# Attention inside a fused kernel: blocks of 64 queries of two heads, Q block-diagonal, and V products over two tiles of queries at once

## The chip, the cores and the metric

The kernel runs on one core of a Trainium2 chip. The metric is device microseconds of one execution; the kernel before takes 874.42 us (median of 3 runs, 874.38 to 879.89).

## The reference

Three steps follow each other. First comes attention for 4 batches and 8 heads over 576 tokens of 64 numbers, in which a query sees all keys of its own block of 64 tokens and of the blocks before it. Then each of the 2304 tokens (512 numbers) is sent to one of 8 experts or skipped, and last comes a dense layer of width 2048. The attention is what the change touches:

```python
scores = scale * np.matmul(q, k.transpose(0, 1, 3, 2))
mask = (pos[:, None] // 64) >= (pos[None, :] // 64)
scores = np.where(mask, scores, -1000000000.0)
scores = scores - np.max(scores, axis=-1, keepdims=True)
attn = np.exp(scores)
attn = attn / (np.sum(attn, axis=-1, keepdims=True) + 1e-09)
return np.matmul(attn, v).astype(np.float32)
```

## The kernel before

The attention works on 16 pairs of heads (4 batches by 4 pairs), one pair after the other, with the stages of neighbouring pairs overlapped. The 576 tokens of a pair are cut into four tiles of 128 (tiles 0 to 3) and a last one of 64 (tile 4). Engines: TensorE (PE) does every product and transpose, VectorE (DVE) and ScalarE (ACT) take results out of PSUM, GpSimd (POOL) does small fills and the scattered writes of the routing, and SyncE (SP) issues the large transfers.

For each pair, `load` brings Q, K and V in (three buffers each), and `tr` turns Q and K over on PE (four transposes each, line 201), so that the two heads lie one above the other: head 0 on partitions 0 to 63, head 1 on 64 to 127. `split_qk` writes each as a high and a low part (lines 212 to 216), and scores are the sum of three products of such parts (line 236). `sc` makes the scores of one tile: for tile i the 128 queries of one head against the first n = 128(i+1) keys, three products for head 0 and three for head 1; each contracts over the 64 numbers of a head, so uses one half of the rows of the array. As a tile holds two blocks of 64, its first 64 queries may not see its last 64 keys; a product in bf16 of two small constants, `top` and `neg`, adds -2^30 there (line 238). Tile 4 is made otherwise: `qd` holds its 64 queries of both heads block-diagonally (head 0 in rows 0 to 63 and columns 0 to 63, head 1 in the other quarter, zeros elsewhere), so that one product with all 128 rows gives both heads (line 242).

`row_max` (line 249) takes the maximum of each row of a tile, `expo` (line 266) the exponential with its sum, head by head. `ptr` transposes the exponentials back in pieces of 128 by 128 (20 transposes per pair for tiles 3 to 0, line 296) and copies them to SBUF, mostly on ACT (line 274). `pv` multiplies them with V (line 315): for tile i and each block of 128 keys, one product for each head, with 64 columns of V stationary and 128 queries moving; the two heads write different halves of PSUM. An f32 product of this kind is two instructions, so that a pair has 40 of them. `pv` of tile 4 is line 308. `norm` and `xout` bring the result into the order of tokens.

The order is set by `OFF` and `at`: each step has a place on a line of 5 steps per pair (scores at 0, maximum 0.3, exponential 0.8, transposes 1.7, V product 2.5 steps after the start of a tile; tiles in the order 4, 3, 2, 1, 0; Q's transposes 3.6 steps ahead of the pair's first scores, the transposes of the 64-token tail 1.6 ahead, Q's and K's loads 10 and 9.5 ahead). That order gives priorities; a planner with its own costs arranges the instructions of each engine by them, and on the chip each engine runs its list in that order. From the 88th step on the order written is taken as it stands. Score tiles have two PSUM buffers (`ps_s`), transposes and small results share three (`ps_m`), the V product has one (`ps_o`). After the attention its buffers are given back, and only then do the weights of the third expert and later ones stream in through SP.

Of the kernel before, what the change touches and what calls it, by code (L numbers as in the profile page):

```python
# [9 lines left out]
F32 = mybir.dt.float32  # L10
F32R = mybir.dt.float32r
# [36 lines left out]
def tile_kernel(ctx: ExitStack, tc: tile.TileContext, q, k, v, w_skip, w_gate, w1, w2, w_in, w_out, alpha, out):  # L48
# [98 lines left out]
    top = acst.tile([128, 128], BF16, name="top")  # L147
    nc.vector.memset(top, 0.0)
    for r in (0, 64):
        nc.vector.memset(top[r:r + 1, 0:64], 1.0)  # L150
    neg = acst.tile([128, 64], BF16, name="neg")
    nc.vector.memset(neg, NEG)
# [33 lines left out]
    def load(p, nm, src):  # L186
        b, h0 = p // NP, p % NP * 2
        a = ld.tile([128, 5, 2, D], F32, tag=nm + "r", name=nm + "r")
# [9 lines left out]
    def tr(p, nm):  # L198
        ps = ps_m.tile([128, 512], F32, tag="m", name="ps" + nm)
        for t in range(4):  # L200
            nc.tensor.transpose(ps[:, t * 128:t * 128 + 128], tok4(p, nm, t), ident)
        for c in "hl":
            st[p][nm + c] = tp.tile([128, 512 if nm == "q" else S], F32R, tag=nm + c, name=nm + c)
# [14 lines left out]
    def tr_tail(p):  # L218
# [3 lines left out]
        for x, hs in enumerate(half):  # L222
            split_qk("q", *(qd[p % 2][hs, c, x * 64:x * 64 + 64] for c in range(2)), ps[hs, 0, :])
# [33 lines left out]
    def expo(p, i):  # L257
# [796 lines left out]
```

## Time and profile before

| | before |
|---|---|
| median of 3 runs | 874.42 us |
| profiled execution, time | 874.04 us |
| profiled execution, span | 872.4 us |
| PE busy | 809.5 us, 93% |
| DVE busy | 460.5 us, 53% |
| ACT busy | 302.8 us, 35% |
| POOL busy | 195.2 us, 22% |
| HBM read and written | 73.20 MB and 11.71 MB |

The span is that of the profiled execution, from its first instruction to its last; 1.6 us of its time lie outside. Busy times are over the whole span, in which the attention is the first 256 us, the experts follow until about 440 us and the dense layer takes the rest. The end of a matmul is modelled in this profile, so where times of PE are added up, starts are taken from starts.

### The profile page before, as it was taken

To read this page: it belongs to the slowest core of one execution; us is meant where nothing else is said; L and a number is where in the kernel's file an instruction comes from. 1 tells how busy PE (TensorE), PEld (TensorE's weight loads), DVE (VectorE), ACT (ScalarE), POOL (GpSimd) and SP (SyncE) were. 2 spreads that over 40 slices of the span, in tenths; PEclk is the share of its full clock that TensorE was granted. 3 is DMA by queue.
4 is the path that set the end of the run, shared out by engine and by line. 5 is a ranking of instruction groups with operands and counts; after the bars stand their busy time and mean duration, and the time that the engine had idled before them with its cause. 6 is when DMAs were issued, how large, how long until landed. Compare 5 with 4: busy or idle time off the path is not lost.

```text
span 872.4 us, 15135 instructions
## 1 busy us (share of the span) xinstructions
PE 809.5 (93%) x5804; PEld 622.0 (71%) x5804; DVE 460.5 (53%) x931; ACT 302.8 (35%) x793; POOL 195.2 (22%) x225
## 2 busy tenths in 40 slices
PE   7999999999995699999489987999999999999998
PEld 4777777777763565775268765788888888888897
DVE  4565757658555566798449999322322222222232
ACT  3766666666750222212134344311121112111121
POOL 1000110110204122323025556222122221212232
PEclk7999999999998799999699999999999999999999
DMA  6664354363314777784733222100020001000000
GB/s 126 163 190 131 85 138 108 84 164 104 98 56 109 242 234 252 235 285 133 235 114 120 89 72 73 48 1 1 1 97 1 1 1 48 25 1 1 25 25 25
DMA packets 96380, 85.86 MB, mean 98 GB/s; under 512 B 68601, under 2 KB 73913, under 8 KB 96272
## 3 DMA queue, kind: packets, MB, share of 16 engines
q1 hardware_dynamic: 93776, 78.88, 30.8%
q0 software_dynamic: 2496, 5.61, 2.1%
q8 instruction: 60, 0.98, 0.4%
q14 instruction: 48, 0.39, 0.2%
HBM read 73.20 MB, written 11.71 MB: 97 GB/s over the span
## 4 chain that ended last, share of the span: by engine, by line
PE 37%; DVE 12%; DMA 9%; issue 3%; ACT 1%; POOL 1%; SPq 0%; DVEq 0%; ACTq 0%; POOLq 0%
PE psf L955 18%; PE psa L988 6%; PE psa L987 6%; PE psa L997 6%; DMA w1t<-in_moe_w_dram 3%; DMA w2t<-in_moe_w_dram 3%; DVE dt L627 2%; DVE gt L966 2%; DMA dr<-in_moe_w_in_dram 2%; DVE dr L628 1%; DVE dt L631 1%; DVE dt L630 1%; DMA dr<-in_moe_w_out_dram 1%; DVE dt L629 1%; DVE wlo L618 1%
## 5 line engine op out<-in xcount | busy, mean ns | idle before, releaser
L955 PE MATMUL psf<-xs,whi 128*128 128x512 f32 (+1 forms) x640 | 160.6, 373 | 6.1 <-ACT xs L842 6.1
L973 POOL TENSOR_TENSOR gl<-gt,gh 128x512 fp32r<-128x512 f32 (+1 forms) x72 | 85.3, 1185 | 249.3 <-PE psa L997 135.9
L955 PEld LDWEIGHTS psf<-xs,whi 128*128 128x128 f32 x640 | 114.7, 188 | 31.3 <-ACT xs L842 6.7
L972 ACT ACTIVATE gh<-gt 128x512 fp32r<-128x512 f32 (+1 forms) x80 | 47.1, 588 | 255.5 <-PE psa L988 150.0
L968 DVE TENSOR_SCALAR gu<-psf,alf 128x512 f32<-128x512 f32 (+1 forms) x64 | 43.7, 683 | 165.2 <-PE psf L955 165.0
L955 PE MATMUL psf<-xs,wlo 128*128 128x512 f32 (+1 forms) x320 | 80.6, 374 | 0.0
L266 ACT ACTIVATE pe<-pss,mx 128x512 f32<-128x512 f32 (+3 forms) x128 | 66.4, 523 | 12.0 <-DVE mx L249 10.1
L249 DVE TENSOR_REDUCE mx<-pss 128x2 f32<-128x1024 f32 (+1 forms) x64 | 52.5, 820 | 31.2 <-PE pss L238 29.3
L955 PEld LDWEIGHTS psf<-xs,wlo 128*128 128x128 f32 x320 | 57.2, 189 | 12.0
L274 ACT ACTIVATE pt<-pspt 128x512 f32<-128x512 f32 (+3 forms) x112 | 52.0, 488 | 34.3 <-PE pspt L296 33.0
L987 PE MATMUL psa<-whi,gh 128*128 128x512 f32 x144 | 57.5, 400 | 4.0 <-ACT gh L972 4.0
L315 PE MATMUL pso<-pt,vr 128*64 128x128 f32 x640 | 59.7, 285 | 0.6 <-ACT pt L274 0.5
L987 PE MATMUL psa<-wkg,gh 128*128 128x512 f32 x144 | 56.8, 394 | 1.5 <-ACT gh L972 1.5
L988 PE MATMUL psa<-wlo,gh 128*128 128x512 f32 x144 | 56.3, 391 | 0.0
L988 PE MATMUL psa<-wkg,gh 128*128 128x512 f32 x144 | 56.2, 390 | 0.0
L296 PE MATMUL pspt<-ident,pe 128*128 128x128 f32 x320 | 52.5, 286 | 0.0
L969 DVE SCALAR_TENSOR_TENSOR gt<-psf,gu 128x512 f32<-128x512 f32 (+1 forms) x64 | 40.0, 625 | 11.5 <-POOL gl L973 5.4
L315 PEld LDWEIGHTS pso<-pt,vr 128*64 128x64 f32 x640 | 39.2, 136 | 9.5 <-issue 3.1
L843 DVE TENSOR_TENSOR xs<-psx,xs 128x512 fp32r<-128x512 f32 x18 | 12.4, 690 | 56.9 <-ACT xs L842 56.9
L296 PEld LDWEIGHTS pspt<-ident,pe 128*128 128x128 f32 x320 | 34.1, 140 | 11.1 <-issue 9.6
L627 DVE TENSOR_SCALAR dt<-dr 128x512 int32<-128x512 int32 x29 | 24.3, 838 | 33.2 <-DMA dr<-in_moe_w_in_dram 28.9
L692 PE MATMUL psh<-w1t,xts 128*32 128x256 f32 x256 | 21.1, 473 | 22.0 <-DMA w1t<-in_moe_w_dram 10.5
(237 smaller groups left out, 1470.3 us busy)
## 6 DMA issues: line engine op xcount, KB each, us to landing
w1t<-in_moe_w_dram SPq DMA_DIRECT2D x32, 512.0 KB
w2t<-in_moe_w_dram SPq DMA_DIRECT2D x32, 512.0 KB
dr<-in_moe_w_in_dram SPq DMA_DIRECT2D x16, 512.0 KB
dr<-in_moe_w_out_dram SPq DMA_DIRECT2D x16, 512.0 KB
out_dram<-ob SPq DMA_DIRECT2D x18, 256.0 KB
qr<-in_q_dram SPq DMA_DIRECT2D x32, 128.0 KB
kr<-in_k_dram SPq DMA_DIRECT2D x32, 128.0 KB
vr<-in_v_dram SPq DMA_DIRECT2D x32, 128.0 KB
```

What stands on the lines that cost most here:

```text
L249: nc.vector.tensor_reduce(out=m, in_=ps[:, :, 0:128 * i + 128], axis=AX.X, op=ALU.max, negate=True)
L266: ins = nc.scalar.activation(out=pt[:, x, 0:n], in_=ps[:, x, 0:n], func=AF.Exp, bias=m[:, x:x + 1], scale=1.0, accum_out=d["sum"][:, x * 4 ...
L274: nc.scalar.activation(out=o, in_=a, func=AF.Copy)
L296: nc.tensor.transpose(ps[:, y, j, :], e[:, x, j * 128:j * 128 + 128], ident)
L315: nc.tensor.matmul(d["o"][hs, i * 128:i * 128 + 128], v5[:, j, x, :], d["pt", i][:, x, j, :], start=(j == 0), stop=(j == i))
L955: nc.tensor.matmul(ps[:, 0:n], wsp[f // 4 * 4 + kk][a][:, ws], c[:, kk, 0:n], start=(n0 == 0 and kk == 0), stop=(n0 == 2 and kk == 3))
L968: nc.vector.tensor_scalar(out=u[:, 0:n], in0=ps[:, 0:n], scalar1=0.0, scalar2=alf[:, f:f + 1], op0=ALU.min, op1=ALU.mult)
L972: nc.scalar.activation(out=hi[:, 0:n], in_=t[:, 0:n], func=AF.Copy)
L973: (nc.gpsimd if w or f % 2 else nc.vector).tensor_tensor(out=lo[:, 0:n], in0=t[:, 0:n], in1=hi[:, 0:n].bitcast(F32), op=ALU.subtract)
L987: nc.tensor.matmul(o, hi[:, ts], whi, start=(f == 0), stop=False)
L988: nc.tensor.matmul(o, hi[:, ts], wlo, start=False, stop=False)
L997: nc.tensor.matmul(acc[w, t], lo[:, t * 128:t * 128 + 128], whi, start=False, stop=False)
```

## The change

Scores are now made in blocks of 64 queries of both heads. `qd`, the block-diagonal store, holds all nine blocks of a pair, with zeros written once at the start on POOL (2 by 2304 numbers per partition, where it was 2 by 256). `tr` of Q writes it in four instructions, two on ACT and two on DVE, each for the 64 partitions of one head, where it was one of each for 128. In `sc`, tile i consists of blocks 2i and 2i+1 (y = 0 and 1): three products of 128 rows for n = 128i+128 keys and three for n = 128i+64, so that no key that a query may not see is computed, and the product with `top` and `neg` goes. `row_max` and `expo` run by block, with the width of that block. The 64 keys that block 2i leaves out are filled with zeros in its exponentials by POOL (four fills a pair), so that the transposes stay as they were.

In `pv` the transposed exponentials of tiles 3 and 2 share one store, and those of 1 and 0 another; products for tile 3 and 1 alone go, and with tile 2 (and 0) one product covers 256 queries for each key block that both tiles have, and 128 for the last. The pair has 24 instructions on that line where it had 40. The result lies in another order of tiles, which `xout`, `weigh_all` and `route_last` follow. `norm` has four small copies where it had three. Q and K keep two load buffers instead of three.

```diff
-        a = ld.tile([128, 5, 2, D], F32, tag=nm + "r", name=nm + "r")
+        a = ld.tile([128, 5, 2, D], F32, tag=nm + "r", name=nm + "r", bufs=3 if nm == "v" else 2)
...
+        if nm == "q":
+            for x, hs in enumerate(half):
+                split_qk("q", *(qd[p % 2][hs, c, 0:8, x] for c in range(2)), ps[hs].rearrange("p (b n) -> p b n", b=8))
+            return
...
-    qd = [acst.tile([128, 2, 128], F32R, name=f"qd{n}") for n in range(2)]
+    qd = [acst.tile([128, 2, NB, 2, 64], F32R, name=f"qd{n}") for n in range(2)]
...
+        q2 = lambda a, blk: qd[p % 2][:, int(a == "ql"), blk].rearrange("p x n -> p (x n)")
         if i < 4:
-            n = 128 * i + 128
-            qc = slice(i * 128, i * 128 + 128)
-            for k, (a, b) in enumerate(PARTS):
-                for x, hs in enumerate(half):
-                    nc.tensor.matmul(ps[:, x, 0:n], d[a][hs, qc], d[b][hs, 0:n], start=(k == 0), stop=False)
-            for x, hs in enumerate(half):
-                nc.tensor.matmul(ps[:, x, n - 64:n], top[hs], neg[hs], start=False, stop=True)
+            for y in (1, 0):
+                n = 128 * i + 64 + 64 * y
+                for k, (a, b) in enumerate(PARTS):
+                    nc.tensor.matmul(ps[:, y, 0:n], q2(a, 2 * i + y), d[b][:, 0:n], start=(k == 0), stop=(k == 2))
...
-            nc.vector.tensor_reduce(out=m, in_=ps[:, :, 0:128 * i + 128], axis=AX.X, op=ALU.max, negate=True)
+            for y in (1, 0):
+                nc.vector.tensor_reduce(out=m[:, y:y + 1], in_=ps[:, y, 0:128 * i + 64 + 64 * y], axis=AX.X, op=ALU.max, negate=True)
...
-            n = 128 * i + 128
-            for x in range(2):
-                ins = nc.scalar.activation(out=pt[:, x, 0:n], in_=ps[:, x, 0:n], func=AF.Exp, bias=m[:, x:x + 1], scale=1.0, accum_out=d["sum"][:, x * 4 + i:x * 4 + i + 1])
+            nc.gpsimd.memset(pt[:, 0, 128 * i + 64:128 * i + 128], 0.0)
+            for y in (1, 0):
+                n = 128 * i + 64 + 64 * y
+                ins = nc.scalar.activation(out=pt[:, y, 0:n], in_=ps[:, y, 0:n], func=AF.Exp, bias=m[:, y:y + 1], scale=1.0, accum_out=d["sum"][:, 2 * i + y:2 * i + y + 1])
...
-        o = d["pt", i] = ptp.tile([128, 2, i + 1, 128], F32, tag="pt", name="pt", padded_shape=[128, 2, 4, 128])
+        g, first = i // 2, i % 2
+        if first:
+            n = 7 if g else 3
+            d["pt", g] = ptp.tile([128, n, 2, 2, 64], F32, tag=f"pt{'ab'[1 - g]}", name="pt", bufs=1 + g)
+        o = d["pt", g]
...
+            r = slice(1 - first, 2 * i + 2 - first, 2)
+            copy((f"{i}{'ab'[xs[0]]}" if i > 1 else str(i)) in ON_ACT, o[:, r, xs[0]:xs[-1] + 1].rearrange("p n y x c -> p y n (x c)"), ps)
...
-        for j in range(i + 1):
+        c0 = 256 - i * 128
+        pt = d.pop(("pt", i // 2))
+        for j in range(i + 2):
+            n = 2 if j <= i else 1
             for x, hs in enumerate(half):
-                nc.tensor.matmul(d["o"][hs, i * 128:i * 128 + 128], v5[:, j, x, :], d["pt", i][:, x, j, :], start=(j == 0), stop=(j == i))
+                nc.tensor.matmul(d["o"][hs, c0:c0 + n * 128], v5[:, j, x, :], pt[:, 2 * j:2 * j + n, :, x].rearrange("p n y c -> p (n y) c"), start=(j == 0), stop=(j == i + 1))
```

## Rows read from the trace of the kernel before

**Rows 1.** The page: engines' busy time, and PE's granted clock in 40 slices.
```profile
PE 809.5 (93%) x5804; PEld 622.0 (71%) x5804; DVE 460.5 (53%) x931; ACT 302.8 (35%) x793; POOL 195.2 (22%) x225
...
PEclk7999999999998799999699999999999999999999
```

**Rows 2.** Table by stretch: us, busy us (instructions) of PE, PEld, DVE, ACT, POOL; clock; DMA.
```profile
120.00:140.00 20.00, 19.55 (x183) 14.41 (x183) 13.27 (x27) 13.44 (x41) 1.16 (x2) 1.00 0.37 89
...
200.00:220.00 20.00, 19.96 (x244) 15.11 (x243) 15.72 (x60) 13.17 (x43) 1.36 (x6) 1.00 0.37 105
```

**Rows 3.** PE's timeline from 119.87 us: start, duration, line, shape, count, [idle before].
```profile
119.87 0.50 PE L236 MATMUL pss<-kh,qh 64*128 64x512 f32 x2
...
123.52 0.66 PE L339 MATMUL psx<-ident,xt 128*128 128x128 f32 x4 [0.23 <-DVE xt L276]
...
125.71 0.95 PE L308 MATMUL pso<-pt,vr 128*64 128x64 f32 x20
126.59 1.09 PE L296 MATMUL pspt<-ident,pe 128*128 128x128 f32 x8
```

**Rows 4.** PE's timeline from 131.90 us on, ending one pair after rows 3 began.
```profile
131.90 0.66 PE L296 MATMUL pspt<-ident,pe 128*128 128x128 f32 x4
132.31 0.48 PE L242 MATMUL pss<-kh,qd 128*128 128x512 f32 x1
132.63 0.40 PE L242 MATMUL pss<-kl,qd 128*128 128x512 f32 x1
132.86 0.42 PE L242 MATMUL pss<-kh,qd 128*128 128x512 f32 x2
133.12 0.28 PE L242 MATMUL pss<-kl,qd 128*128 128x64 f32 x1
133.23 0.28 PE L242 MATMUL pss<-kh,qd 128*128 128x64 f32 x1
133.44 0.66 PE L315 MATMUL pso<-pt,vr 128*64 128x128 f32 x8
134.02 0.44 PE L296 MATMUL pspt<-ident,pe 128*128 128x128 f32 x2
134.39 0.50 PE L236 MATMUL pss<-kh,qh 64*128 64x512 f32 x2
134.73 0.39 PE L236 MATMUL pss<-kl,qh 64*128 64x512 f32 x2
134.96 0.39 PE L236 MATMUL pss<-kh,ql 64*128 64x512 f32 x2
135.20 0.20 PE L238 MATMUL pss<-neg,top 64*128 64x64 bf16 x2
135.33 0.66 PE L201 MATMUL psq<-ident,qr 128*128 128x128 f32 x4
135.92 0.44 PE L315 MATMUL pso<-pt,vr 128*64 128x128 f32 x4
```

**Rows 5.** Groups by shape, 0 to 250 us: busy us, mean ns, idle before.
```profile
L249 DVE TENSOR_REDUCE mx<-pss 128x2 f32<-128x1024 f32 x16 | 19.6, 1225 | 14.7 <-PE pss L238 14.6
...
L214 DVE SCALAR_TENSOR_TENSOR ql<-psq,qh 128x512 fp32r<-128x512 f32 x16 | 11.1, 691 | 5.0 <-ACT qh L212 4.7
...
L249 DVE TENSOR_REDUCE mx<-pss 128x2 f32<-128x256 f32 x15 | 6.3, 423 | 9.4 <-PE pss L238 9.4
...
L212 ACT ACTIVATE qh<-psq 128x512 fp32r<-128x512 f32 x16 | 9.6, 597 | 11.1 <-PE psq L201 11.1
...
L369 POOL MEMSET lw<- 128x72 f32 x4 | 0.6, 156 | 8.0 <-DVE l L409 8.0
...
L208 POOL MEMSET qd<- 128x256 f32 x2 | 0.5, 302 | 0.0
```

**Rows 6.** PE's timeline, the last result of the attention.
```profile
256.08 0.66 PE L339 MATMUL psx<-ident,xt 128*128 128x128 f32 x4 [0.80 <-DVE xt L276]
```

**Rows 7.** SP's timeline, the first weights issued after the attention.
```profile
275.50 6.26 SPq L79 DMA_DIRECT2D w2t<-in_moe_w_dram  x4
```

More of the change, by code (lines that the diff above doesn't have):

```diff
@@ L146, in tile_kernel @@
     nc.vector.tensor_scalar(out=tlo, in0=tok, scalar1=63, scalar2=None, op0=ALU.bitwise_and)
[L147 to L152, printed above, removed]
     thi = acst.tile([128, 5], F32, name="thi")
@@ L201, in tr @@
             nc.tensor.transpose(ps[:, t * 128:t * 128 + 128], tok4(p, nm, t), ident)
+        if nm == "q":
+            for x, hs in enumerate(half):
+                split_qk("q", *(qd[p % 2][hs, c, 0:8, x] for c in range(2)), ps[hs].rearrange("p (b n) -> p b n", b=8))
+            return
         for c in "hl":
-            st[p][nm + c] = tp.tile([128, 512 if nm == "q" else S], F32R, tag=nm + c, name=nm + c)
+            st[p][nm + c] = tp.tile([128, S], F32R, tag=nm + c, name=nm + c)
         split_qk(nm, *(st[p][nm + c][:, 0:512] for c in "hl"), ps)
-    qd = [acst.tile([128, 2, 128], F32R, name=f"qd{n}") for n in range(2)]
+    qd = [acst.tile([128, 2, NB, 2, 64], F32R, name=f"qd{n}") for n in range(2)]
     for n in range(2):
@@ L222, in tr_tail @@
         for x, hs in enumerate(half):
-            split_qk("q", *(qd[p % 2][hs, c, x * 64:x * 64 + 64] for c in range(2)), ps[hs, 0, :])
+            split_qk("q", *(qd[p % 2][hs, c, 8, x] for c in range(2)), ps[hs, 0, :])
         split_qk("k", *(st[p]["k" + c][:, 512:S] for c in "hl"), ps[:, 1, :])
@@ L241, in sc @@
                 for k, (a, b) in enumerate(PARTS):
-                    nc.tensor.matmul(o, qd[p % 2][:, int(a == "ql")], d[b][:, c], start=(k == 0), stop=(k == 2))
+                    nc.tensor.matmul(o, q2(a, 8), d[b][:, c], start=(k == 0), stop=(k == 2))
     def row_max(p, i):
@@ L296, in ptr @@
                     nc.tensor.transpose(ps[:, y, j, :], e[:, x, j * 128:j * 128 + 128], ident)
-            copy((f"{i}{'ab'[xs[0]]}" if i > 1 else str(i)) in ON_ACT, o[:, xs[0]:xs[-1] + 1], ps)
+            r = slice(1 - first, 2 * i + 2 - first, 2)
+            copy((f"{i}{'ab'[xs[0]]}" if i > 1 else str(i)) in ON_ACT, o[:, r, xs[0]:xs[-1] + 1].rearrange("p n y x c -> p y n (x c)"), ps)
     def pv(p, i):
@@ L327, in norm @@
         nc.vector.reciprocal(out=r, in_=r)
-        nc.vector.tensor_copy(out=rb[b][:, 0:4, hp, :], in_=r[:, 0:8].rearrange("p (x t) -> p t x", x=2))
         for x, hs in enumerate(half):
-            nc.vector.tensor_copy(out=rb[b][0:64, 4, hp, x:x + 1], in_=r[hs, 8:9])
+            for y, rows in enumerate(half):
+                n = 5 - y
+                nc.vector.tensor_copy(out=rb[b][rows, 0:n, hp, x:x + 1], in_=r[hs, y:9:2].unsqueeze(2))
     def xout(p):
@@ L338, in xout @@
         for t in range(4):
-            nc.tensor.transpose(ps[:, t].rearrange("p h d -> p (h d)"), xt[:, t * 128:t * 128 + 128], ident)
+            nc.tensor.transpose(ps[:, t].rearrange("p h d -> p (h d)"), xt[:, 384 - t * 128:512 - t * 128], ident)
         if hp % 2 == 0:
@@ L385, in weigh_all @@
         for t in range(4):
-            nc.tensor.transpose(ps[:, t, 0:n].rearrange("p h c -> p (h c)"), lg[0:n * 32, t * 128:t * 128 + 128], ident[0:n * 32, 0:n * 32])
+            nc.tensor.transpose(ps[:, t, 0:n].rearrange("p h c -> p (h c)"), lg[0:n * 32, 384 - t * 128:512 - t * 128], ident[0:n * 32, 0:n * 32])
         for t in range(4):
@@ L397, in route_last @@
             kk = 128 if t < 4 else 64
-            nc.tensor.matmul(ps[0:kk, t, 0], xts[b * NP + hp][:, t * 128:t * 128 + kk], wbd[:, hp, 0:18], start=True, stop=True)
+            c0 = 384 - t * 128 if t < 4 else 512
+            nc.tensor.matmul(ps[0:kk, t, 0], xts[b * NP + hp][:, c0:c0 + kk], wbd[:, hp, 0:18], start=True, stop=True)
         f = rb[b][:, 0:4, hp].unsqueeze(3).to_broadcast([128, 4, 2, 9])
```

4 lines of the change are left out of this document (3 added, 1 removed).

## The prediction

> **What bounds the kernel now.** I read the page first, then a table by stretch, then PE's timeline of one pair, then the groups by shape, and last how the attention ends and what starts after it. On the page PE is busy for 93% of the span and no other engine for more than 53%, and PE's granted clock stands in its top tenth in the slices of the steady attention [rows 1]; the table gives it there as 1.00, the 2.4 GHz level [rows 2]. In those stretches PE is busy for 19.55 and 19.96 of 20 us, DVE for 13.27 and 15.72, ACT for some 13.4, POOL for about 1 [rows 2]. So PE sets the pace of the attention. The busy share does not say whether PE streams or drains, so I add starts.
>
> One pair lasts from 119.87 to 134.39, the same product of tile 3 in both rows: 14.52 us [rows 3, 4]. There are 16 such pairs, and the routing lies among them. Within a stretch of equal shapes a transpose costs 0.11: two transposes between other work take 0.37 (134.02 to 134.39), four take 0.59 (135.33 to 135.92), hence 0.11 each and a constant of 0.15 [rows 4]. Eight V instructions take 0.58 (133.44 to 134.02): four couples of heads at 0.11 and again a constant of 0.14 [rows 4]. This constant is what a reader should see: it appears where PE passes between products of 128 rows and columns (transposes, tile 4's scores), products of 64 rows (the other scores) and products of 64 columns (V). Where transposes pass to tile 4's scores it is missing: 131.90 to 133.44 holds four transposes, three products of 512 at 0.23 and three of 64 at 0.11, 1.46 in all, against 1.54 shown with an entry and an exit in it [rows 4]. From 119.87 to 134.39 the timeline passes 21 times between the three kinds, rows 3 giving the first and rows 4 the last.
>
> **The change, part by part.** All figures are per pair in us unless said.
>
> Scores, streaming. Two heads of 64 rows run side by side: both products of 512 (134.73) are followed by the next two after 0.23, which is what one product of 128 rows takes (132.63 to 132.86) [rows 4]. So before, tiles 3 to 0 cost three times 0.23, 0.17, 0.12 and 0.11: by columns at 0.45 ns, with 0.11 as the floor (133.12 to 133.23) [rows 4]; together 1.89. After, the blocks run one behind the other: 512, 448, 384, 320, 256, 192, 128 and 64 columns at 0.23, 0.20, 0.17, 0.14, 0.12 and three times 0.11, 1.19 for each of three parts, 3.57. That adds 1.68. The Trainium skill, "TensorEngine Tiling (Array Packing)", section "Theoretical Speedup", says that splitting the array's rows for contractions of at most 64 gives up to 2x; by it alone this change gives half of the array away, and the sum would be these 1.68 a pair, 25 us more in 15 pairs. The rows agree on the streaming, and the rest of the sum is what that rule leaves out.
>
> Masks. Four couples go. One takes 0.13 up to the next work (135.20 to 135.33) [rows 4], of which I count 0.07 as its own, the rest is the way out of the stretch: -0.28.
>
> Switches. The first score after a switch also takes 0.34 instead of 0.23 (134.39 to 134.73) [rows 4], 0.05 above the constant; six such entries fall away, -0.30. In the order of the steps, after the change, only V of tiles 0 and 1, V of tile 4, the 64-row transposes of the tail, and V of tiles 2 and 3 interrupt the full shape: 8 switches instead of 21, -13 x 0.15 = -1.95. Before, that written order has 16; the planner made 21 by cutting V of tile 3 and scores in pieces. A cut of V in the new order costs two switches, 0.30.
>
> V products. Columns stay: 20 couples of 128 (2.20) become 8 of 256 and 4 of 128, the same at equal price per column. The moving operand now lies in runs of 64. Bounds: nothing, or the price of separate products of 64, (0.88 - 0.25)/10 = 0.06 against 0.055 from tile 4's V (125.71 to 126.59, of which I count 0.25 as its constant and the way to its last products of 64 rows) [rows 3], +0.2. I take nothing, as a couple of 256 issues fewer instructions.
>
> Sum: +1.68 - 0.28 - 0.30 - 1.95 = -0.85. Adding the whole pair as a test: 38 transposes 4.18, V 2.20, V of tile 4 0.88, tile 4's scores 1.02, tail 0.2, scores 1.89, masks 0.28, twenty switches 3.0 (one is in the 0.88), entries 0.30, the wait for the copied result 0.23 [rows 3]: 14.18 of 14.52. The missing 0.34 is couples broken by other work, which can't happen to blocks, and small waits. Against that I allow one cut of V at 0.30. I take -0.8; ends: -1.4 (no cut, no leftover waits) and 0 (three cuts).
>
> DVE. Q's low part takes two instructions of 0.69 instead of one; eight maxima replace four: from 1225 ns for 1024 columns and 423 for 256 a column costs 1.04 ns and an instruction 0.16 [rows 5], so 4 x 0.16 more less 256 columns, +0.37; one small copy in norm, 0.15 at most. Together +1.2. ACT: one more instruction of 0.60 [rows 5], less narrower exponentials. Both lie beside PE's work. If the cover goes, PE waits for maxima or copies: this is a rival below. Latency per tile does not grow, as the exponential of one block can start while the next block is still multiplied.
>
> POOL. Four fills a pair, each below the 156 ns of a fill of 72 columns [rows 5], are covered by the exponentials that run at the same time. They stand in POOL's queue with the tokens that release weight loads and with the list writes, which wait for K or an exponential; what is behind them then is a fill, and behind that PE's transposes, planned 0.9 step later than the exponential. Bounds 0 to 0.6; I take 0. Filling the larger store at the start: 302 ns for 256 columns, 156 for 72 [rows 5], 0.8 ns a column, 1.9 us each, once, before PE has turned Q over a second time; 0.
>
> Loads. With two buffers Q of the pair after next can be issued once the tail of the pair using that buffer is turned over, eight steps (some 23 us) ahead of its own transposes; SP issues in order, so a waiting Q load holds V loads and weights behind it. Bounds 0 and one late load; I take 0.
>
> Ends. At the start nothing overlaps Q's second instructions: up to 0.60 + 0.69 [rows 5], taken +0.8. At the end the last V product comes in one group and its copy is waited for as today (0.80) [rows 6]: +0.3. The weights after the attention are issued at 275.50, behind its end [rows 7], so that the later stages move with it and the gain is kept whole.
>
> The pairs at the two ends overlap only half, so 15 x -0.8 = -12.0; with the ends -10.9. The profiled execution takes 874.04, 1.6 outside its span of 872.4; the median is 0.4 above it. **874.0 - 10.9 = 863.**
>
> **Rivals.**
> 1. *A larger gain.* V is never cut, and the leftover waits go as well: -1.4 x 15 + 1 = -20, 854. For it: five stretches of one kind merge into one another. Against it: the planner cut V before.
> 2. *DVE (with ACT) becomes the bound.* Scaled to a pair, DVE has 9.6 to 11.4 us of work [rows 2], with 1.2 more 10.8 to 12.6, in a pair of 13.7: 79 to 92%. With queues in order and the routing in bursts, PE then waits on maxima and the gain shrinks to between 0 and 0.4 a pair: 869 to 875. Against it: ACT and DVE have a fifth of their time free away from the routing.
> 3. *Slower: the switches stay.* V's group needs the last copies of tile 2 (or 0), and the planner may cut it into pieces and put scores between. Place: V against the full shape; price 0.30 a cut. From three cuts a pair the gain is gone; with all 21 switches it is -0.85 + 1.95 = +1.1 a pair, 874 + 16.5 + 1 = 892; with five cuts +0.65, 885. The skill's rule named above points this way too. For it: today's 16 became 21. Against it: most of those cuts were scores, which are now of one shape with the transposes.
>
> **How the numbers follow.** About 1%, 8.7 us, is what can be told from no change. Forecast, 857 to 870: 0.55, two thirds of it faster by over 1%, as the bound lies at 865.7. Rival 1: 0.18. Rival 2: 0.15, within 1%. Rival 3: 0.12, nearly all slower by over 1%. Faster: 0.37 + 0.18 = 0.55; same 0.18 + 0.15 + 0.01 = 0.34; slower 0.11. The range takes most of rival 1 and rival 2 and leaves the far end of rival 3: 850 to 878.
>
> **What would show it.** One pair of PE's timeline should hold 8 to 12 stretches and last some 13.7; tiles' scores as 128-row products 0.23 apart for 512 columns, with no constant beside transposes; V in groups of 16 and 8 instructions, about 1.7 and 0.8 with their constants; the list of waits with little of DVE or POOL before PE. Wrong would be: a gap between transposes and block scores, V in four or more pieces, PE idle behind a maximum or a fill, or a first weight issued after the attention that doesn't move with its end.

## The result and the profile after

The changed kernel takes 881.26 us (median of 15 runs, 879.36 to 887.01) and the kernel before, run beside it, 876.35 (15 runs): a ratio of 1.0058, with a 95% interval of 1.0037 to 1.0079. The forecast was 863 us with a range of 850 to 878, so it was wrong, and in its sign. The profiled execution took 882.70 us, with a span of 881.1.

The page of the kernel after, the line of busy times and that of PE's granted clock, answering to [rows 1]:

```profile
PE 797.8 (91%) x5420; PEld 623.5 (71%) x5420; DVE 480.8 (55%) x1023; ACT 311.9 (35%) x809; POOL 207.3 (24%) x289
...
PEclk7999999999997899999699999899999999999999
```

PE has 11.7 us less to do than before and the span is 8.7 us longer: the gain in work is there, and more than all of it has gone into idle time. The table by stretch of the kernel after (us, then busy us and instructions of PE, PEld, DVE, ACT, POOL; clock; DMA), in the two stretches of [rows 2]:

```profile
120.00:140.00 20.00, 18.54 (x156) 14.90 (x152) 12.79 (x35) 13.44 (x41) 3.05 (x9) 1.00 0.43 101
200.00:220.00 20.00, 18.99 (x186) 14.83 (x186) 15.83 (x61) 13.30 (x39) 1.17 (x8) 1.00 0.45 128
```

The granted clock is 1.00 in both stretches, as before, so there it is not the clock. PE was idle for 0.45 and 0.04 of these 20 us; now it is idle for 1.46 and 1.01. PE's timeline of one pair of the kernel after (start, duration, line, shape, count, [idle before <- what ended it]) shows where:

```profile
64.56 0.66 PE L348 MATMUL psx<-ident,xt 128*128 128x128 f32 x4 [0.22 <-ACT pt L272]
...
67.10 0.95 PE L311 MATMUL pso<-pt,vr 128*64 128x64 f32 x20 [0.58 <-DVE xr L355]
...
71.49 1.74 PE L323 MATMUL pso<-pt,vr 128*64 128x256 f32 x16 [0.66 <-ACT pt L272]
73.16 0.66 PE L298 MATMUL pspt<-ident,pe 128*128 128x128 f32 x4
...
74.59 0.44 PE L298 MATMUL pspt<-ident,pe 128*128 128x128 f32 x2
74.79 0.47 PE L234 MATMUL pss<-kh,qd 128*128 128x512 f32 x1
75.10 0.39 PE L234 MATMUL pss<-kl,qd 128*128 128x512 f32 x1
75.33 0.60 PE L234 MATMUL pss<-kh,qd 128*128 128x512 f32 x2
75.76 0.36 PE L234 MATMUL pss<-kl,qd 128*128 128x448 f32 x1
...
76.70 0.87 PE L323 MATMUL pso<-pt,vr 128*64 128x256 f32 x8
77.50 0.66 PE L283 MATMUL pspt<-ident,p 128*128 128x128 f32 x4
...
79.45 0.33 PE L348 MATMUL psx<-ident,xt 128*128 128x128 f32 x1 [0.22 <-ACT pt L272]
```

This pair lasts 14.89 us (64.56 to 79.45), and 13.43 of them are PE's own work. Two waits are new: 0.58 before V of tile 4, for DVE's `xr`, and 0.66 before V of tiles 3 and 2, for ACT's copy of transposes. The pair of [rows 3] passed V of tile 4 without a wait (125.71), but only just, as DVE's timeline of the kernel before shows; the second part of `xr` ends at 125.71 there:

```profile
125.44 0.27 DVE L347 TENSOR_TENSOR xr<-psx,rb 64x128 f32<-64x128 f32 x1
```

DVE's timeline of the kernel after, ahead of the first wait, tells what made `xr` late:

```profile
62.73 0.68 DVE L212 SCALAR_TENSOR_TENSOR qd<-psq,qd 64x512 fp32r<-64x512 f32 x1
63.34 0.67 DVE L274 COPY xt<-pso 128x512 f32<-128x512 f32 x1
63.94 0.67 DVE L274 COPY pt<-pspt 128x512 f32<-128x512 f32 x1
64.64 0.69 DVE L212 SCALAR_TENSOR_TENSOR qd<-psq,qd 64x512 fp32r<-64x512 f32 x1
65.37 0.95 DVE L246 TENSOR_REDUCE mx<-pss 128x1 f32<-128x384 f32 x2
66.35 0.69 DVE L355 TENSOR_TENSOR xr<-psx,rb 128x512 f32<-128x512 f32 x1
```

From 62.73 on DVE has no pause: the second half of Q's low part (64.64, 0.69 us) stands ahead of two maxima and of `xr`. V of tile 4 needs one of the three shared PSUM buffers (`ps_m`), and the one it gets is held by the transposes that `xr` (66.35) reads. So the 0.58 at PE is most of that 0.69; the first run below takes it away. An instruction on 64 partitions costs what one on 128 does: 0.68 and 0.69 here, 691 ns before [rows 5]. For the second wait, ACT's timeline of the kernel after:

```profile
70.56 0.87 ACT L272 ACTIVATE pt<-pspt 128x384 f32<-128x384 f32 x2
```

Both copies of tile 2 run on ACT (70.56), the second right behind the first, and the group of 16 V instructions starts at 71.49 when the later is done. Before, V of tile 3 ran by itself ahead of these copies, and V of tile 2 began without a wait, as PE's timeline of the kernel before shows:

```profile
130.85 1.12 PE L315 MATMUL pso<-pt,vr 128*64 128x128 f32 x12
```

The list of waits from 20 to 240 us of the kernel after (who waits, for whom: us in total, times, longest; PEld is PE's load of a stationary operand, which waits just ahead of its product):

```profile
POOL pe L261 <- PE pspt L298: 80.7, 47, 3.4
...
PEld pso L311 <- DVE xr L355: 9.1, 13, 0.8
...
PEld pso L323 <- ACT pt L272: 5.4, 7, 0.8
```

The first wait comes in 13 pairs, the second in 7. POOL's fills wait for PE for 80.7 us in all, and no row has PE waiting for a fill. Finally the end of the attention, from PE's timeline, and the first weights behind it, from SP's, of the kernel after:

```profile
263.19 0.66 PE L348 MATMUL psx<-ident,xt 128*128 128x128 f32 x4 [0.79 <-DVE xt L274]
```
```profile
283.00 1.02 SPq L79 DMA_DIRECT2D w2t<-in_moe_w_dram  x2
```

The attention ends 7.1 us later than in [rows 6] and the weights start 7.5 later than in [rows 7]; the span is 8.7 longer, so most of the loss lies in the attention. Of its 7.1 us, 1.1 come before the first result (34.76 instead of 33.69). Over 12 pairs (second to fourteenth result) a pair takes 15.67 us on average instead of 15.20; idle time of PE in it is 1.40 instead of 0.18, and the rest 14.27 instead of 15.02.

### The profile page after: what moved, and what is told of

It is laid out like the page before. It is cut to its first block, busy times and chain, and to the rows that moved or that the text cites. A ratio compares the mean times of both kernels' runs of the same rounds, so it can differ in the third digit from the quotient of the medians.

```text
span 881.1 us, 14573 instructions
## 1 busy us (share of the span) xinstructions
PE 797.8 (91%) x5420; PEld 623.5 (71%) x5420; DVE 480.8 (55%) x1023; ACT 311.9 (35%) x809; POOL 207.3 (24%) x289
## 4 chain that ended last, share of the span: by engine, by line
PE 51%; DVE 19%; DMA 12%; ACT 9%; issue 4%; SPq 1%; POOL 1%; another core or an unknown queue 1%; DVEq 0%; ACTq 0%; POOLq 0%
PE psf L965 18%; PE psa L998 6%; PE psa L997 6%; PE psa L1007 6%; DMA w1t<-in_moe_w_dram 4%; DMA w2t<-in_moe_w_dram 4%; PE pss L234 4%; ACT pe L264 3%; PE pso L323 3%; ACT pt L272 3%; DMA dr<-in_moe_w_in_dram 2%; PE pspt L298 2%; DVE mx L246 2%; DVE dt L637 2%; ACT qd L210 2%
## 5 line engine op out<-in xcount | busy, mean ns | idle before, releaser
L234 PE MATMUL pss<-kh,qd 128*128 128x512 f32 (+7 forms) x256 | 76.0, 340 | 2.5 <-ACT pe L264 2.1
L264 ACT ACTIVATE pe<-pss,mx 128x512 f32<-128x512 f32 (+7 forms) x128 | 63.2, 498 | 10.5 <-DVE mx L246 8.1
L246 DVE TENSOR_REDUCE mx<-pss 128x1 f32<-128x512 f32 (+7 forms) x128 | 53.4, 449 | 19.6 <-PE pss L234 18.4
L234 PEld LDWEIGHTS pss<-kh,qd 128*128 128x128 f32 x256 | 47.0, 192 | 7.4 <-ACT pe L264 3.5
L323 PE MATMUL pso<-pt,vr 128*64 128x256 f32 (+1 forms) x384 | 41.7, 352 | 6.0 <-ACT pt L272 6.0
L979 DVE SCALAR_TENSOR_TENSOR gt<-psf,gu 128x512 f32<-128x512 f32 (+1 forms) x64 | 40.0, 625 | 10.2 <-POOL gl L983 4.0
```

The lines of the kernel that those rows point to most:

```text
L234: nc.tensor.matmul(ps[:, y, 0:n], q2(a, 2 * i + y), d[b][:, 0:n], start=(k == 0), stop=(k == 2))
L246: nc.vector.tensor_reduce(out=m[:, y:y + 1], in_=ps[:, y, 0:128 * i + 64 + 64 * y], axis=AX.X, op=ALU.max, negate=True)
L264: ins = nc.scalar.activation(out=pt[:, y, 0:n], in_=ps[:, y, 0:n], func=AF.Exp, bias=m[:, y:y + 1], scale=1.0, accum_out=d["sum"][:, 2 * i ...
L323: nc.tensor.matmul(d["o"][hs, c0:c0 + n * 128], v5[:, j, x, :], pt[:, 2 * j:2 * j + n, :, x].rearrange("p n y c -> p (n y) c"), start=(j = ...
```

## The experiments

Theory: what PE saves is lost to Q's second instructions, which delay `xr` and the maxima on DVE and copies on ACT. Rivals: the blocks themselves cost PE more than forecast, the V groups wait for copies whatever Q does, or the PSUM buffer, not engine time, is what Q's second instructions use up. All ratios are to the kernel before on the same chip, with 95% intervals. "Pair" is the distance between the third and fourth result on PE, idle time of PE that within this pair, and "passages" counts how often PE passes in it between the three kinds of products that the prediction names. "First" and "last" are the times at which PE starts the first and the sixteenth result, in the one profiled execution of each run.

| run | ratio | interval | pair, us | idle, us | passages | first, us | last, us |
|---|---|---|---|---|---|---|---|
| before | 1 | | 14.52 | 0.22 | 21 | 33.69 | 256.08 |
| after | 1.0058 | 1.0037 to 1.0079 | 14.89 | 1.45 | 8 | 34.76 | 263.19 |
| e1_q_once | 0.9877 | 0.9850 to 0.9904 | 13.93 | 0.80 | 8 | 32.72 | 248.25 |
| e14_act_twice | 0.9926 | 0.9901 to 0.9952 | 14.05 | 0.80 | 8 | 33.31 | 250.25 |
| e15_dve_twice | 1.0015 | 0.9989 to 1.0042 | 14.86 | 1.46 | 8 | 32.36 | 258.94 |
| e10_q_second_from_sbuf | 1.0009 | 0.9985 to 1.0033 | 14.89 | 1.50 | 8 | 32.13 | 258.07 |
| e9_before_q_halves | 1.0144 | 1.0105 to 1.0183 | 15.35 | 1.00 | 21 | 34.44 | 269.47 |
| e4_v_groups_only | 0.9869 | 0.9848 to 0.9890 | 13.57 | 0.36 | 14 | 32.34 | 243.48 |
| e16_v_groups_2b | 0.9874 | 0.9831 to 0.9916 | 13.19 | 0.36 | 14 | 32.63 | 243.08 |
| e8_v_groups_swapped | 0.9872 | 0.9832 to 0.9912 | 13.12 | 0.00 | 16 | 38.51 | 253.68 |
| e3_blocks_only | 1.0184 | 1.0164 to 1.0204 | 15.31 | 1.17 | 12 | 35.28 | 271.42 |
| e13_blocks_pool | 0.9902 | 0.9864 to 0.9940 | 14.34 | 0.51 | 12 | 30.05 | 248.90 |
| e2_copies_swapped | 0.9987 | 0.9959 to 1.0015 | 14.10 | 0.76 | 8 | 35.47 | 259.43 |
| e6_q_by_pool | 0.9846 | 0.9803 to 0.9890 | 13.93 | 0.80 | 8 | 28.56 | 243.66 |
| e7_q_by_dma | 1.0117 | 1.0075 to 1.0158 | 13.44 | 0.61 | 10 | 34.79 | 272.22 |
| e11_pool_swapped | 0.9803 | 0.9767 to 0.9839 | 13.42 | 0.25 | 8 | 28.79 | 241.00 |
| e12_pool_2b | 0.9786 | 0.9741 to 0.9832 | 13.53 | 0.41 | 8 | 29.15 | 240.95 |

**Q's second instructions.** The first run takes them out of the changed kernel:

```diff
-            for x, hs in enumerate(half):
-                split_qk("q", *(qd[p % 2][hs, c, 0:8, x] for c in range(2)), ps[hs].rearrange("p (b n) -> p b n", b=8))
+            split_qk("q", *(qd[p % 2][:, c, 0:8, 0] for c in range(2)), ps.rearrange("p (b n) -> p b n", b=8))
```

> The changed kernel, but Q's high and low part are each written by one instruction for all 128 partitions into the same half of the block-diagonal store, so that the two heads' queries mix (the separation of the heads is left out; PE's work is the same). Theory A (PE waits for DVE and ACT): DVE reaches the copy of the result (xr) 0.69 us earlier and the 0.58 us that PE waits for it in each pair goes: 881 - 9 = 872 us. Theory B (block scores and V groups cost PE more than was priced): no change, 881 us.

Measured 868.69 us, 0.9877. Two instructions a pair, one on each engine and both off the path by their engines' busy shares, cost 1.8% (1.0058 against 0.9877), three times the loss that was to be explained. In PE's timeline of this run only one wait is left in the pair, that for tile 2's copies, as long as in the kernel after; so this one belongs to the V groups and not to Q:

```profile
66.93 1.74 PE L322 MATMUL pso<-pt,vr 128*64 128x256 f32 x16 [0.66 <-ACT pt L271]
```

The next run puts Q's second instructions into the kernel before, where nothing else is changed:

```diff
-        split_qk(nm, *(st[p][nm + c][:, 0:512] for c in "hl"), ps)
+        for hs in half if nm == "q" else [slice(0, 128)]:
+            split_qk(nm, *(st[p][nm + c][hs, 0:512] for c in "hl"), ps[hs])
```

> The kernel before with Q's high and low part written by two instructions each for 64 partitions, nothing else changed. Theory A (DVE is on PE's path at xr): xr ends at 125.71 in the kernel before, just when PE starts the product that needs its PSUM buffer, so that DVE's 0.69 more a pair shows almost whole: +0.4 to +0.6 a pair, 884 to 887 us, 1.007 to 1.010 of before. Rival (the halves cost only together with the blocks' additional maxima): no change, within 0.3%.

Measured 890.24 us, 1.0144, more than I expected. DVE's timeline of this run, the kernel before with Q in halves, shows the same picture as that of the kernel after:

```profile
65.62 0.69 DVE L215 SCALAR_TENSOR_TENSOR ql<-psq,qh 64x512 fp32r<-64x512 f32 x1
66.34 0.96 DVE L250 TENSOR_REDUCE mx<-pss 128x2 f32<-128x768 f32 x1
67.33 0.69 DVE L347 TENSOR_TENSOR xr<-psx,rb 128x512 f32<-128x512 f32 x1
```

And PE's timeline of the same run waits twice in the pair, for a copy on ACT and for `xr`:

```profile
65.45 0.66 PE L340 MATMUL psx<-ident,xt 128*128 128x128 f32 x4 [0.62 <-ACT pt L275]
...
68.08 0.95 PE L309 MATMUL pso<-pt,vr 128*64 128x64 f32 x20 [0.37 <-DVE xr L347]
```

So the cost does not need the blocks: a schedule in which `xr` came just in time has no room for 0.69 us ahead of it. Two runs divide it between the engines, each with one instruction on one of them for all 128 partitions and two on the other:

```diff
             for x, hs in enumerate(half):
-                split_qk("q", *(qd[p % 2][hs, c, 0:8, x] for c in range(2)), ps[hs].rearrange("p (b n) -> p b n", b=8))
+                nc.scalar.activation(out=qd[p % 2][hs, 0, 0:8, x], in_=pv_(ps[hs]), func=AF.Copy, scale=0.125)
+            for x, hs in full:        # full = [(0, slice(0, 128))]; in e15 it stands above, and half here
+                nc.vector.scalar_tensor_tensor(out=qd[p % 2][hs, 1, 0:8, x], in0=pv_(ps[hs]), scalar=0.125, in1=qd[p % 2][hs, 0, 0:8, 0].bitcast(F32), op0=ALU.mult, op1=ALU.subtract)
```

> The changed kernel with Q's high part written by two instructions on ACT as it is there, the low part by one on DVE for all 128 partitions (the heads' separation is left out). If it is DVE's 0.69 a pair that PE waits for, this takes the time of e1, 867 to 870 us, 0.988 of before; if it is ACT's 0.60, that of the changed kernel, 880 to 883, 1.006; if both count, 873 to 877.

> The reverse: the high part by one instruction on ACT, the low part by two on DVE (the heads' separation is left out). If it is DVE's 0.69 a pair that PE waits for, the time of the changed kernel, 880 to 883 us, 1.006 of before; if ACT's 0.60, that of e1, 867 to 870, 0.988; if both count, 873 to 877.

Measured 871.35 us, 0.9926, and 880.66, 1.0015. Against e1, ACT's second instruction costs 0.5% and DVE's 1.4%, in sum about the 1.8% of both. With DVE's alone the idle time is back at 1.46. One more run keeps the engine time of both and lets the PSUM buffer go, as the second instructions read SBUF:

```diff
-            for x, hs in enumerate(half):
-                split_qk("q", *(qd[p % 2][hs, c, 0:8, x] for c in range(2)), ps[hs].rearrange("p (b n) -> p b n", b=8))
+            split_qk("q", *(qd[p % 2][:, c, 0:8, 0] for c in range(2)), ps.rearrange("p (b n) -> p b n", b=8))
+            hs = half[1]
+            hi, lo = (qd[p % 2][hs, c, 0:8] for c in range(2))
+            nc.scalar.activation(out=hi[:, :, 1], in_=hi[:, :, 0].bitcast(F32), func=AF.Copy, scale=0.125)
+            nc.vector.scalar_tensor_tensor(out=lo[:, :, 1], in0=hi[:, :, 0].bitcast(F32), scalar=0.125, in1=hi[:, :, 1].bitcast(F32), op0=ALU.mult, op1=ALU.subtract)
```

> The changed kernel with as many instructions for Q on ACT and DVE as it has, but the first of each covers all 128 partitions and reads PSUM, and the second, for 64 partitions, reads SBUF (the heads' separation is left out). Theory A1 (the second instructions hold one of the three shared PSUM buffers longer, and PE waits for a buffer): the time of e1, 0.988 of before, 867 to 870 us. Theory A2 (it is DVE's and ACT's time, 0.69 and 0.60 a pair ahead of what PE waits for): that of the changed kernel, 1.006, 880 to 884 us. In between, the share of each.

Measured 879.85 us, 1.0009, between the two theories. The steady pair is that of the kernel after (14.89 us, of which 1.50 idle instead of 1.45), so in it the engines' time counts, and letting the buffer go earlier gains nothing. This run is 0.5% faster than the kernel after all the same. In the profiled executions its attention ends 5.1 us earlier, of which 2.6 come before the first result; whether the PSUM buffer has a part in that is not shown.

**V and the blocks, each alone.** The kernel before with the V groups (and two load buffers for Q and K), its scores and its Q as they were:

```diff
-        o = d["pt", i] = ptp.tile([128, 2, i + 1, 128], F32, tag="pt", name="pt", padded_shape=[128, 2, 4, 128])
+            d["pt", g] = ptp.tile([128, n, 2, 128], F32, tag=f"pt{'ab'[1 - g]}", name="pt", bufs=1 + g)
...
-                nc.tensor.matmul(d["o"][hs, i * 128:i * 128 + 128], v5[:, j, x, :], d["pt", i][:, x, j, :], start=(j == 0), stop=(j == i))
+                nc.tensor.matmul(d["o"][hs, c0:c0 + n * 128], v5[:, j, x, :], pt[:, 2 * j:2 * j + n, x], start=(j == 0), stop=(j == i + 1))
```

> The kernel before with V products for two tiles at once, scores as before (two heads side by side, with the mask product). Theory A: five or six V stretches become two, at 0.30 each -0.9 to -1.2 us a pair, and a wait for tile 2's copies of up to 0.7 comes in: -0.2 to -1 a pair, 876 - 3 to - 15, so 861 to 873 us. Rival C (grouping V is what costs): 876 + 5 to + 10, 881 to 886 us.

Measured 866.6 us, 0.9869. The groups alone gain 1.3%. PE's timeline of this run, from one result to the next:

```profile
59.47 0.65 PE L348 MATMUL psx<-ident,xt 128*128 128x128 f32 x4
...
65.41 2.11 PE L324 MATMUL pso<-pt,vr 128*64 128x256 f32 x16 [0.23 <-ACT pt L274]
...
73.03 0.66 PE L348 MATMUL psx<-ident,xt 128*128 128x128 f32 x4
```

The wait for tile 2's copies is there with 0.23 instead of 0.66, and V of tile 4 waits for nothing. Fourteen passages between kinds remain of 21, and the pair is 0.95 shorter. The blocks without the groups, with Q as in the change:

```diff
-            d["pt", g] = ptp.tile([128, n, 2, 2, 64], F32, tag=f"pt{'ab'[1 - g]}", name="pt", bufs=1 + g)
+        o = d["pt", i] = ptp.tile([128, 2, i + 1, 2, 64], F32, tag="pt", name="pt", padded_shape=[128, 2, 4, 2, 64])
...
-                nc.tensor.matmul(d["o"][hs, c0:c0 + n * 128], v5[:, j, x, :], pt[:, 2 * j:2 * j + n, :, x].rearrange("p n y c -> p (n y) c"), start=(j == 0), stop=(j == i + 1))
+                nc.tensor.matmul(d["o"][hs, c0:c0 + 128], v5[:, j, x, :], pt[:, :, j, x], start=(j == 0), stop=(j == i))
```

> The changed kernel with V products tile by tile as before the change (40 instructions a pair), scores in blocks. Theory A: V of tile 3 no longer waits for tile 2's copies, which gives back up to 0.66 us a pair, but three more V stretches cost six switches at 0.15: 0 to +0.9 a pair, 881 to 890 us. Rival C (grouping V is what costs, since it waits for the later of two tiles): 881 - 10 = 871 us.

Measured 894.51 us, 1.0184, outside what was expected: by itself this half of the change is slower than the whole change. But it holds Q's second instructions. The same with Q spread by POOL (as in e6 below):

> e3 (scores in blocks, V tile by tile) with Q's copies by POOL as in e6. Without the second instructions on ACT and DVE the blocks should cost what they were priced at: per pair +1.68 streaming, -0.28 masks, -0.30 entries, some six fewer switches at 0.15, so 0 to +0.4 a pair; 876 to 883 us, 0.998 to 1.006 of before, where e3 took 1.018. If they cost PE more than priced, 1.01 or above.

Measured 870.23 us, 0.9902, better than I had priced it: the blocks alone, freed of Q's second instructions, gain 1.0%. PE's own part of the pair is 13.83 us (14.34 less 0.51) against 14.30, so that nine passages fewer, with the masks and entries that go, pay for more than the 1.68 us of longer streaming. The rival that the blocks cost too much on PE falls. Not all of the 1.0% lies in the pairs, though: in the profiled executions the attention ends 7.2 us earlier than before, of which 3.6 come before the first result, and from the first to the last result the gain is 3.5 us (218.9 instead of 222.4).

**Q by another engine.** POOL was busy for 1 to 3 of 20 us. It can spread Q into the block-diagonal store from a dense copy that ACT and DVE write as before:

```diff
+            hl = [tp.tile([128, 512], F32R, tag="q" + c, name="q" + c, bufs=1) for c in "hl"]
+            split_qk("q", *hl, ps)
+            for c, t in enumerate(hl):
+                for x, hs in enumerate(half):
+                    nc.gpsimd.tensor_copy(out=qd[p % 2][hs, c, 0:8, x], in_=t[hs].rearrange("p (b n) -> p b n", b=8))
```

(V's loads go from three buffers to two here, which makes room for the copy.)

> The changed kernel, but Q's high and low part are written by one instruction of ACT and one of DVE for all 128 partitions into plain tiles, and POOL copies them into the block-diagonal store (four copies of 64 partitions by 512 a pair; V has two load buffers, to make room). Theory A (the second half instruction on DVE stands ahead of xr and PE waits for xr): as in e1, 869 us, 0.988 of before. Rival: POOL's copies hold DVE up, or come too late, and PE waits as in the changed kernel: 878 to 882 us.

Measured 864.25 us, 0.9846. POOL's timeline of this run:

```profile
127.49 1.27 POOL L201 CAST qd<-qh 64x512 fp32r<-64x512 f32 x2 [2.22 <-ACT qh L213]
128.83 1.27 POOL L201 CAST qd<-ql 64x512 fp32r<-64x512 f32 x2
```

Four copies of some 0.64 us a pair, and no row of the list of waits has PE waiting for them. The idle time is that of e1, 0.80, so the spreading costs PE nothing here. From first to last result e6 takes 215.1 us and e1 215.5; what it is ahead of e1 (0.9877) comes before the first result, at 28.56 instead of 32.72. V's two load buffers were not tried alone. By DMA instead, four transfers in SP's queue, with nothing else different:

```diff
-                    nc.gpsimd.tensor_copy(out=qd[p % 2][hs, c, 0:8, x], in_=t[hs].rearrange("p (b n) -> p b n", b=8))
+                    nc.sync.dma_start(out=qd[p % 2][hs, c, 0:8, x].bitcast(F32), in_=t[hs].bitcast(F32).rearrange("p (b n) -> p b n", b=8))
```

> As e6, but the four copies a pair into the block-diagonal store are transfers issued by SP. Theory A: 869 us, 0.988 of before. Rival: four more issues a pair in SP's queue hold up Q's, K's and V's loads or the weights: 875 us or more.

Measured 887.97 us, 1.0117, as the rival said. Two lists of waits of this run, SP's own and that of PE's weight loads, from 20 to 240 us:

```profile
SPq L184 <- PE pso L326: 61.1, 11, 8.1
```
```profile
PEld pss L237 <- ACT pe L267: 9.6, 9, 1.7
```

A V load in SP's queue waits for a product (61.1 us in all, 8.1 once; in e6 it is 37.9), and what stands behind it, the copies of Q among it, waits as well. PE then waits 9.6 us for exponentials before scores, and pairs become uneven: the first three last 18.71, 14.53 and 13.44 us, where each lasts 14.9 in the kernel after.

**The wait for tile 2's copies.** In the kernel after, the second copy of tile 2 goes to DVE and a copy of tile 4 to ACT:

```diff
-ON_ACT = ("0", "1", "2a", "2b", "3a", "3b", "5", "xt")
+ON_ACT = ("0", "1", "2a", "3a", "3b", "4", "5", "xt")
```

> The changed kernel with two copies exchanged between engines: the transposed exponentials of tile 4 are copied by ACT instead of DVE, the second half of tile 2's by DVE instead of ACT. Theory A: the first frees 0.67 us of DVE ahead of xr (the 0.58 wait goes), the second lets both halves of tile 2 be copied side by side (0.4 of the 0.66 wait before V of tiles 3 and 2 goes): 15 pairs x 1.0 = -15 us, 866 us; at least below 872. Theory B: no change, 881 us.

Measured 877.16 us, 0.9987. The pair of the table is 0.79 shorter than that of the kernel after, but the time falls by only 0.7%. Both waits are shorter or gone, but PE now waits 0.55 for ACT before the transposes of the result (77.75), where it waited 0.22. A later pair lasts 18.39 us. The same swap in the kernel with V groups alone:

> e4 (scores as before, V in groups) with tile 4's transposed exponentials copied by ACT and the second half of tile 2's by DVE. PE idles 0.3 us a pair in e4 before V of tiles 3 and 2, behind ACT's copies. If it is the last copy alone that it waits for, 0.2 to 0.3 a pair go: 862 to 864 us where e4 took 866.6; if other work takes its place, no change, 866 to 868.

Measured 867.58 us, 0.9872, no better than e4 although its steady pair is 0.45 shorter and has no idle time at all. Here the long pair lasts 20.2 us (178.53 to 198.7). DVE's timeline of this run at its start:

```profile
181.31 0.17 DVE L480 TENSOR_SCALAR pr<-tok 128x5 int32<-128x5 int32 x1 [2.97 <-issue]
181.39 0.95 DVE L249 TENSOR_REDUCE mx<-pss 128x2 f32<-128x768 f32 x1
182.25 0.68 DVE L355 TENSOR_TENSOR xr<-psx,rb 128x512 f32<-128x512 f32 x1
```

PE's timeline of the same run:

```profile
182.99 1.10 PE L312 MATMUL pso<-pt,vr 128*64 128x64 f32 x20 [2.72 <-DVE xr L355]
```

And its table by stretch, columns as above, right after this place:

```profile
186.00:194.00 8.00, 8.00 (x40) 5.47 (x41) 2.91 (x11) 3.80 (x14) 0.00 (x0) 0.51 0.67 194
```

An instruction of the routing (`pr`, which writes a tile that the scattered write of a list reads) stood ahead of the maxima in DVE's queue and began only after 2.97 us; PE was idle for 2.72, and then its granted clock fell to 0.51, near the 1.2 GHz level, from 186 to 194. In e2 the same instruction began at 185.34 after 2.07 us; the chain of waits there has the scattered write (`lst`) ahead of it, and the granted clock is 0.63 from 188 to 196. That `pr` waits for the end of that write is named in DVE's timeline of e11 (below), which has the same instruction at the same place:

```profile
172.71 0.17 DVE L483 TENSOR_SCALAR pr<-tok 128x5 int32<-128x5 int32 x1 [1.93 <-DMA lst<-pr,pi]
```

PE waits 1.74 us for `xr` there (174.38), and its granted clock stays at 1.00 from 170 to 194. So the swap cures the wait that it was made for, and the arrangement of instructions that the planner then makes has a worse one elsewhere. How much of e8's median that costs is not shown: its profiled execution was the slowest of its seven (873.53 us), and of the 10.2 us by which its attention ends later than e4's, 6.2 come before the first result, in a stretch from 10 to 30 us with a granted clock of 0.50. Only the second copy of tile 2 moved, in the kernel with V groups:

```diff
-ON_ACT = ("0", "1", "2a", "2b", "3a", "3b", "5", "xt")
+ON_ACT = ("0", "1", "2a", "3a", "3b", "5", "xt")
```

> e4 (scores as before, V in groups) with the second half of tile 2's transposed exponentials copied by DVE. If the blocks of scores add nothing to the V groups once the waits are gone, this gains as e12 did over e6 (0.6%): 861 us, 0.981 of before, the same as e12. If the blocks are worth something of their own, it stays at e4's 0.987.

Measured 865.98 us, 0.9874, the same as e4 within the intervals. By the expectation the blocks would then be worth something of their own; the traces of the next two runs say where.

**Both cures together.** Q by POOL with the swap, and with the one copy moved:

> e6 (POOL copies Q into the block-diagonal store) with tile 4's transposed exponentials copied by ACT and the second half of tile 2's by DVE. PE idles 0.43 us a pair in e6 before V of tiles 3 and 2 and before V of tile 4. If each is a wait for one late copy, 0.3 a pair go: 860 us, 0.980 of before; if the planner's order changes with it as in e8, no change: 864 to 868.

> e6 with the second half of tile 2's transposed exponentials copied by DVE, and nothing else. ACT's queue is what V of tiles 3 and 2 waits for in e6; DVE has 80% of its time taken: 861 us, 0.981 of before, if DVE is free at that place; 864 to 868 if it is not.

Measured 862.71 us, 0.9803, and 860.3, 0.9786; their intervals overlap. PE's timeline of the second, from one result to the next:

```profile
42.68 0.60 PE L351 MATMUL psx<-ident,xt 128*128 128x128 f32 x4
...
44.63 0.95 PE L314 MATMUL pso<-pt,vr 128*64 128x64 f32 x20
...
48.65 1.73 PE L326 MATMUL pso<-pt,vr 128*64 128x256 f32 x16 [0.28 <-ACT pt L275]
...
56.25 0.60 PE L351 MATMUL psx<-ident,xt 128*128 128x128 f32 x4
```

The wait before V of tile 4 is gone, the other is 0.28 instead of 0.66, and the pair takes 13.57. This version beats both kernels: 2.1% faster than before, by an interval of 1.7 to 2.6%. Beside the V groups with the same copy moved (e16, 0.9874) that is another 0.9%, with intervals that just touch, but the traces do not show it in the pairs. PE's first and last result, from the timelines of e16 and then of e12:

```profile
32.63 0.66 PE L348 MATMUL psx<-ident,xt 128*128 128x128 f32 x4
...
243.08 0.66 PE L348 MATMUL psx<-ident,xt 128*128 128x128 f32 x4 [0.80 <-DVE xt L276]
```
```profile
29.15 0.60 PE L351 MATMUL psx<-ident,xt 128*128 128x128 f32 x4
...
240.95 0.66 PE L351 MATMUL psx<-ident,xt 128*128 128x128 f32 x4 [0.79 <-DVE xt L277]
```

From first to last result e16 takes 210.45 us and e12 211.80. So beside V groups with this copy moved the blocks gain nothing in the pairs; e12 is ahead by 3.48 us before its first result, and its attention ends 2.13 earlier.

## Why the prediction was wrong, step by step

- **Scores, streaming**: right. Products of 512 columns follow each other after 0.23 (75.10 to 75.33), and the next two, 512 and 448, take 0.43 (75.33 to 75.76), the forecast 0.23 and 0.20.
- **Masks and switches**: right. The passages are 8, as forecast. Transposes pass to block scores without a constant: two take 0.20 (74.59 to 74.79). The first product behind them takes 0.31 instead of 0.23, as tile 4's first did before (0.32) [rows 4]. V is not cut: groups of 16 and 8.
- **V products**: right. The groups take 1.67 (71.49 to 73.16) and 0.80 (76.70 to 77.50); by the forecast's prices, six couples of 256, two of 128 and the constant give 1.68, and two of each 0.80. What was left out is that a group starts when the last of its copies is done. Rival 3 names that need, but expects a cut from it; it came as a wait of 0.66.
- **The sum of PE's own work**: right in size. Without idle time a pair is 0.75 us shorter over 12 pairs, where 0.8 was taken.
- **"Both lie beside PE's work"**: this step failed. The sizes were right: over the 12 pairs DVE is busy for 11.02 us a pair instead of 9.88 and ACT for 10.76 instead of 10.14, +1.14 and +0.63 where 1.2 and 0.60 were taken. But they were taken to cost nothing. The idle time of PE rose by 1.22 a pair, and 1.22 - 0.75 = +0.47 is the loss; times 12 it is 5.6 of the 7.1 us by which the attention ends later. Taking Q's second instructions away gives 1.8% back (e1), DVE's 1.4 and ACT's 0.5 (e14, e15). In e1 the idle time is 0.72 a pair, so 0.68 of the 1.22 are theirs; the other 0.54 stay without them, and the one wait left in e1's steady pair is that of the V group for tile 2's copies, the second term that the sum had at nothing.
- **The forecast's size**: 863 of 874 us is 0.987, and e1 measures 0.9877. That is luck in part: e1 still has 0.72 us of idle time in a pair, and its PE has 14.00 us of work of its own where the kernel after has 14.27.
- **POOL**: right, no wait of PE behind a fill. **Loads**: the list of waits has no row in which PE waits for a late load of Q.
- **Ends**: the first scores come 1.0 us later (12.29 instead of 11.29; 0.8 was taken). The +0.3 at the other end did not come: the last result waits 0.79 where it waited 0.80 [rows 6]. The weights moved with the end, as forecast.
- **Rival 1** did not come. **Rival 2** named the mechanism, DVE with ACT, and missed its size: 869 to 875 was worked out from busy shares. DVE is busy for 11.02 of 15.67 us a pair, 70%, and is not the bound. What counted is the place of 0.69 us in its queue: ahead of an `xr` that was just in time, in front of a PSUM buffer that PE wants next. "A fifth of their time free" says nothing of that. **Rival 3** did not come: the switches went.

The Trainium skill, "Perfetto Trace Analysis", section "Tensor Engine Instruction (MATMUL, LD_WEIGHTS)", says that ACT and DVE run strictly in the order of their queues; the traces agree: `xr` at 66.35 runs behind Q's half at 64.64, and in e8 a maximum behind the 2.97 us of `pr`. The Trainium skill, "TensorEngine Tiling (Array Packing)", section "Key Properties", says that a change of tiling mode drains the engine; e4 agrees, where seven passages fewer come with 0.95 us less a pair, and in e13 the steady pair is 0.18 us shorter although its blocks give half of the array away.

What stays open: the gains in the pairs do not add. From first to last result the V groups take 11.2 us off the kernel before (e4) and the blocks 3.5 (e13), but both together 7.3 (e6), or 10.6 with one copy moved (e12), where the V groups with that copy moved take off 11.9 (e16). The 0.80 us of idle time in e6 against 0.41 in e12 points at tile 2's copies, but the arrangement of all engines differs between the two. Nor was it tried what brings the first result 3.6 to 5.1 us forward in e6, e11, e12 and e13: the blocks, POOL's copies, V's two load buffers, or the granted clock, which from 14 to 18 us is 1.00 in the profiled executions of these four and 0.50 in those of the kernel before and e16.

## What to carry to other kernels

An instruction on an engine with time to spare (DVE is busy 70% here) is not free: look in the timeline at what stands behind it in that queue, by how much that is early, and who holds a buffer until it is done. Cutting an eviction into two by partitions costs a whole one more (0.69 us on DVE, 0.60 on ACT), so give the rearrangement to an engine whose queue nobody waits for. Try the halves of a change alone: here each was a gain of about 1% once the helper instructions of the blocks were out of the way, and these were most of the loss. Then look at where in the trace a gain lies: half of the blocks' came before the first result, and in the pairs they added nothing to the V groups.

## What was not expected of the hardware

While POOL fills the larger `qd` at the start, small DVE instructions on SBUF last about as long as the fill. The rows of the kernel after, DVE's timeline and POOL's:

```profile
2.53 4.28 DVE L146 TENSOR_SCALAR tlo<-tok 128x5 int32<-128x5 int32 x1 [1.13 <-POOL tok L135]
```
```profile
2.64 3.96 POOL L206 MEMSET qd<- 128x2304 f32 x2
```

Before, the same instruction took 0.92 us beside fills of 0.55. The fill itself was estimated well, 1.9 us each for a measured 2.0. POOL's copies of Q in e6, also between SBUF tiles, did not lengthen DVE's instructions that read PSUM beside them: Q's low part took 0.69 and the two copies behind it 0.68. Two small ones on SBUF beside POOL's first copies in e6 (6.55 to 7.85 us) lasted 0.52 and 0.40, where in the kernel after, with no copy beside them, they took 0.17 and 0.11. And one stall of 2.7 us on PE was followed by some 8 us at the lower clock (e8), so that it cost more than twice its own length: that pair took 20.2 us instead of 13.12. The stall of 1.74 us in e11 was followed by none: the clock stayed at 1.00, and that pair took 15.06 instead of 13.42.
